# Two weight loads moved from SP's queue to GpSimd's in a one-core Mish feed-forward kernel

## The chip, the cores and the metric

The kernel runs on one core of a Trainium2 chip. The core has five engines with an instruction stream each: TensorE (PE, matmuls and, as PEld, their weight loads), VectorE (DVE), ScalarE (ACT), GpSimd (POOL) and SyncE (SP), which here only issues DMAs and waits. The engines run side by side and meet at semaphores. The metric is the device time of one execution in microseconds (us).

## The reference

With x of 2048 x 512, w1 of 512 x 1792 and w2 of 1792 x 512, all in bf16:

```
h   = einsum("bsd,df->bsf", x, w1) + b1
sp  = log1p(exp(-abs(h))) + where(h > 0, h, 0)      # softplus
act = h * tanh(sp)                                  # Mish
out = einsum("bsf,fd->bsd", act, w2)
```

So two matrix products with an elementwise Mish and a bias between them.

## The kernel before

**Tiles.** The 512 rows of w1 are 4 "k" tiles of 128, and the 1792 columns are 14 "f" tiles of 128. The 2048 tokens go in four blocks of 512 (BLOCKS), or 16 tiles of 128. The first product needs x with its 512 features on the partitions (xT) and gives h transposed: for each f tile, four matmuls over k collect in a bank of PSUM (line 192, `mm1_step`), and ACT applies Mish with the bias and writes a_sb (line 198). The second product takes a_sb as weights and w2 as the moving operand, 14 matmuls a token tile (line 249, `mm2`). ACT, or DVE for the last tile, copies the result out (lines 233 and 236), and a DMA stores it.

**Ten tokens apart.** For the last ten tokens (fewer f tiles of two of them) DVE computes h itself as 120 dot products (`dots`, line 211) from w1T and xv, with its own loads. ACT does their Mish late (line 223), just before the last token tile.

**The start.** PE opens with six dummy matmuls on constants (WARM, line 155). x's first two token tiles come in their natural layout (x_nat, one DMA each); PE transposes them against an identity (line 169), and DVE copies the result to xT (line 171). The identity is made by GpSimd: a memset of ones and one affine_select (lines 145 and 147). The rest of x arrives already transposed by the DMA. To have work early, PE goes through the first f tiles piece by piece, in the order of arrival:

```
transpose_x(0, ...)                 # x's token tile 0
first(0, 0)                         # k 0, f tiles 0-3, token tile 0
transpose_x(1, ...)                 # token tile 1
first(0, 1); first(1, 0); first(1, 1)
# then k 2 and 3 of f tiles 0-3, all k of f tiles 4-7, on token tiles 0-1 together;
# then token tiles 2-3 of f tiles 0-7, and from there whole blocks
```

`first(j, k)` is four matmuls of 128 columns. Each step waits for its own piece of w1 by a semaphore (`t_w1[k, f]`, in `mm1_step`), so an order that is fixed in the program meets loads that land when they land.

**Loads.** All are on line 92 of `load`, and the queue is the engine that issues: ACT issues k 0 of f tiles 0-3 and then b1; SP issues everything else, one after the other, in the order of the program. The first on SP are x_nat 0, x_nat 1, then k 1 (128 KB) and k 2-3 (256 KB) of f tiles 0-3, the two halves of f tiles 4-7 (256 KB each), the transposing load of tokens 256-511, the two halves of f tiles 8-13, w2, and then what DVE's dots and the later blocks need. Nothing on SP waits until the first store. The f tiles come in the groups (0, 4), (4, 8) and (8, 14) (GROUPS), and `load_w1(q, ks, a, b)` loads k range ks of f tiles a to b from queue q. GpSimd issues no DMA; it is done when the identity is.

Of the kernel before, what the change touches and what calls it, by code (L numbers as in the profile page):

```python
# [7 lines left out]
GROUPS = ((0, 4), (4, 8), (8, 14))  # L8
# [26 lines left out]
def bass_standalone__dense_activation_mish__prompt_kernel(  # L35
# [14 lines left out]
    KT, FT = D // P, F // P  # L50
# [7 lines left out]
    with ExitStack() as es:  # L58
# [22 lines left out]
        def sem(name):  # L81
            return es.enter_context(nc.semaphore(name))
# [5 lines left out]
        pool = Stream(nc.gpsimd, sem("c_pool"))  # L88

        def load(q, dst, src, name, transpose=False):  # L90
            s = sem(name)
            (q.eng.dma_start_transpose if transpose else q.eng.dma_start)(dst, src).then_inc(s, 16)  # L92
            return (s, 16)
# [3 lines left out]
        def load_w1(q, ks, a, b):  # L97
            t = load(q, w1_sb[:, ks, a * P:b * P], w1v[:, ks, a * P:b * P], "s_w1_%d_%d" % (ks.start, a))
            for f in range(a, b):
                for k in range(ks.start, ks.stop):  # L100
                    t_w1[k, f] = t
# [6 lines left out]
        def load_xT(lo, hi):  # L108
            t = load(sp, xT[:, :, lo:hi], x2[lo:hi, :], "s_xT%d" % lo, True)
            for j in range(lo // P, hi // P):  # L110
                t_xT[j] = t
# [15 lines left out]
        for a, b in GROUPS:  # L127
            if a == F0:
                load_xT(2 * P, 4 * P)
            for ks in (slice(0, 1), slice(1, 2), slice(2, KT)) if a == 0 else (slice(0, 2), slice(2, KT)):  # L130
                load_w1(act if (a, ks.start) == (0, 0) else sp, ks, a, b)
        t_b1 = load(act, b1_nat[:, :], b1.rearrange("(j p) -> j p", p=P), "s_b1")
        load_w2(0, 5)
# [8 lines left out]
        for s in range(2, len(BLOCKS)):  # L142
# [3 lines left out]
        pool.wait(t_ones)  # L146
        t_id = pool.mark(pool.eng.affine_select(ident[:, :], ones[:, :], pattern=[[1, P]], compare_op=ALU.is_equal,  # L147
                                                fill=0.0, base=0, channel_multiplier=-1))
        act.eng.preload_act_table(ACT.Mish)  # L149

        c_w = nc.const_aps.tensor(1.0, [P, P], BF)
# [177 lines left out]
```

## Time and profile before

| | us |
|---|---|
| median of 3 runs | 105.33 (105.02 to 105.4) |
| the profiled execution | 105.21 |
| its span, first to last instruction | 103.9 |
| PE busy | 100.9 |
| DVE busy | 77.1 |
| ACT busy | 48.1 |
| POOL busy | 0.7 |
| first matmul on k 1 of f tiles 0-3 | 5.16 from the span's start |

In the views of the profile, times count from the span's start. The timeline gives start and length; SPq and ACTq are the sequencers of SP and ACT issuing a DMA, and the length of such a row is the issue alone, not the transfer. The list of DMA issues gives the time from the start of the issue to the landing of the data, as a median where it groups several. In the table by stage, each row is a stretch, its length, the busy time of each engine with the count of instructions, the granted clock of TensorE, the mean busy share of the 16 DMA engines (which can count a little over 1) and what they moved in GB/s. The program calls w1 and w2 w_sb in these rows alike.

### The profile page before, as it was taken

The numbers are of one execution on the slowest core, as the hardware profiler recorded it, in microseconds if no ns is written. First come the engines' busy times: TensorE is split into PE (matmuls) and PEld (weight loads), VectorE is DVE, ScalarE is ACT, GpSimd is POOL, SyncE is SP. The second block draws the span as 40 slices with busy tenths as digits, with TensorE's granted clock in tenths as the row PEclk, the third lists the DMA queues.
The fourth block names the chain that finished last, engine by engine and source line by source line (L and its number), as shares of the span: only waits on it lengthen the run. The fifth ranks groups of instructions, "written<-read, shape, count | busy, mean of one in ns | idle before, by whom it ended". The sixth has DMA issues, their size and how long they took to land.

```text
span 103.9 us, 1471 instructions
## 1 busy us (share of the span) xinstructions
PE 100.9 (97%) x532; PEld 50.9 (49%) x532; DVE 77.1 (74%) x257; ACT 48.1 (46%) x75; POOL 0.7 (1%) x6
## 2 busy tenths in 40 slices
PE   6899999999999999999999999999999999999992
PEld 2598744444444444444444444444444444444482
DVE  0530000599999999999999999999999999990011
ACT  1303998112247777222227777522117778720220
POOL 2000000000000000000000000000000000000000
PEclk9999999999999999999999999999999999999999
DMA  2899999999999800010111000001111000001111
GB/s 76 244 304 349 348 367 188 357 289 207 154 244 250 266 8 0 0 50 2 48 50 50 3 0 6 3 0 50 50 50 50 0 0 0 0 6 50 50 50 51
DMA packets 21267, 11.11 MB, mean 107 GB/s; under 512 B 15372, under 2 KB 21004, under 8 KB 21260
## 3 DMA queue, kind: packets, MB, share of 16 engines
q1 hardware_dynamic: 20944, 10.86, 39.8%
q10 hardware_dynamic: 316, 0.16, 0.5%
q8 instruction: 4, 0.07, 0.3%
q14 instruction: 3, 0.02, 0.1%
HBM read 5.25 MB, written 2.10 MB: 71 GB/s over the span
## 4 chain that ended last, share of the span: by engine, by line
PE 93%; DMA 3%; SPq 1%; ACT 0%; issue 0%
PE ps L192 47%; PE ps L249 47%; DMA w_sb<-in_w_dram 3%; SPq L92 1%; ACT o_sb L233 0%
## 5 line engine op out<-in xcount | busy, mean ns | idle before, releaser
L211 DVE SCALAR_TENSOR_TENSOR prod<-w1T,xv 128x512 f32<-128x512 bf16 x120 | 73.6, 684 | 13.1 <-DMA w1T<-in_w_dram 13.1
L192 PE MATMUL ps<-xT,w_sb 128*128 128x512 bf16 (+4 forms) x264 | 49.6, 350 | 0.4 <-DMA w_sb<-in_w_dram 0.4
L249 PE MATMUL ps<-w_sb,a_sb 128*128 128x512 bf16 (+3 forms) x252 | 49.1, 355 | 0.0
L198 ACT ACTIVATE a_sb<-ps,b_sb 128x512 bf16<-128x512 f32 (+2 forms) x56 | 37.3, 691 | 14.0 <-PE ps L192 14.0
L192 PEld LDWEIGHTS ps<-xT,w_sb 128*128 128x128 bf16 x264 | 25.5, 100 | 23.7 <-DMA w_sb<-in_w_dram 0.7
L249 PEld LDWEIGHTS ps<-w_sb,a_sb 128*128 128x128 bf16 x252 | 23.6, 98 | 25.1
L233 ACT ACTIVATE o_sb<-ps 128x512 bf16<-128x512 f32 (+1 forms) x16 | 9.2, 576 | 38.2 <-PE ps L249 38.2
L211 DVE DVE_READ_ACCUMULATOR prod<-w1T,xv 128x1 f32 x120 | 9.6, 80 | 0.0
L236 DVE CAST o_sb<-ps 128x256 bf16<-128x256 f32 (+1 forms) x2 | 0.8, 375 | 7.7 <-PE ps L249 7.7
L155 PE MATMUL ps<-const-bfloat16-1.0 128*128 128x512 bf16 (+2 forms) x8 | 2.8, 498 | 0.8 <-PEq L314 0.8
L171 DVE COPY xT<-ps 128x128 bf16<-128x128 bf16 (+1 forms) x6 | 1.2, 245 | 2.9 <-PE ps L169 2.9
L149 ACT ACT_TABLE_LOAD x1 | 1.3, 1283 | 2.1 <-issue 2.1
L155 PEld LDWEIGHTS ps<-const-bfloat16-1.0 128*128 128x128 bf16 x8 | 1.0, 136 | 1.9 <-issue 1.9
L169 PE MATMUL ps<-ident,x_nat 128*128 128x128 bf16 x8 | 1.3, 311 | 0.0
L169 PEld LDWEIGHTS ps<-ident,x_nat 128*128 128x128 bf16 x8 | 0.9, 142 | 0.3 <-DMA x_nat<-in_x_dram 0.3
L273 DVE STREAM_TRANSPOSE b_t<-b_pad 32x32 bf16<-32x32 bf16 x4 | 0.8, 202 | 0.1
L123 DVE MEMSET b_pad<- 32x64 uint32 x1 | 0.1, 112 | 0.9 <-PEq L314 0.9
L219 DVE TENSOR_TENSOR hb<-hv,b_sb 128x40 f32<-128x40 f32 (+1 forms) x2 | 0.4, 218 | 0.1
L223 ACT ACTIVATE a_sb<-hb 128x40 bf16<-128x40 f32 (+1 forms) x2 | 0.4, 244 | 0.0
L147 POOL TENSOR_SCALAR_AFFINE_SELECT ident<-ones 128x128 bf16<-128x128 bf16 x1 | 0.3, 292 | 0.1
L145 POOL MEMSET ones<- 128x128 bf16 x1 | 0.2, 204 | 0.3 <-POOLq L314 0.3
L275 DVE CAST b_sb<-b_t 128x14 f32<-128x14 bf16 x1 | 0.2, 176 | 0.0
(5 smaller groups left out, 0.6 us busy)
## 6 DMA issues: line engine op xcount, KB each, us to landing
out_dram<-o_sb SPq DMA_DIRECT2D x15, 128.0 KB, 1.7
w_sb<-in_w_dram SPq DMA_DIRECT2D x1, 1152.0 KB, 10.5
w_sb<-in_w_dram SPq DMA_DIRECT2D x3, 256.0 KB, 4.0
w_sb<-in_w_dram SPq DMA_DIRECT2D x2, 384.0 KB, 4.7
xv<-in_x_dram SPq DMA_DIRECT2D x1, 768.0 KB, 7.9
w_sb<-in_w_dram SPq DMA_DIRECT2D x1, 640.0 KB, 6.4
xv<-in_x_dram SPq DMA_DIRECT2D x1, 512.0 KB, 11.0
x_nat<-in_x_dram SPq DMA_DIRECT2D x2, 128.0 KB, 2.3
```

What stands on the lines that cost most here:

```text
L92: (q.eng.dma_start_transpose if transpose else q.eng.dma_start)(dst, src).then_inc(s, 16)
L149: act.eng.preload_act_table(ACT.Mish)
L155: nc.tensor.matmul(ps[:, 3, 0:n], c_w, c_m[:, 0:n], start=True, stop=True)
L169: mm = nc.tensor.transpose(psb[:, i * P:(i + 1) * P], x_nat[:, j, k * P:(k + 1) * P], ident[:, :])
L171: t = dve.mark(nc.vector.tensor_copy(xT[:, ks[0]:ks[0] + n, j * P:(j + 1) * P], psb[:, 0:n * P].rearrange("p (k t) -> p k t", k=n)))
L192: return nc.tensor.matmul(ps[:, bank, lo:hi], w1_sb[:, k, f * P:(f + 1) * P], xT[:, k, starts[s] + lo:starts[s] + hi], start=first, stop=( ...
L198: t = act.mark(act.eng.activation(a_sb[:, f, starts[s]:starts[s] + width(s, f)], ps[:, bank, 0:width(s, f)], ACT.Mish, bias=b1_sb[:, f:f + ...
L211: t_dot[b] = dve.mark(nc.vector.scalar_tensor_tensor(prod[:, b, :], w1T[:, f, :], 1.0, xv[:, v, :], ALU.mult, ALU.mult, accum_out=hv[:, f, ...
L233: t = act.mark(act.eng.activation(o_sb[:, i, lo:hi], ps[:, bank, 0:hi - lo], ACT.Copy))
L236: t = dve.mark(nc.vector.tensor_copy(o_sb[:, i, lo:hi], ps[:, bank, 0:hi - lo]))
L249: mm = nc.tensor.matmul(ps[:, bank, 0:hi - lo], a_sb[:, f, i * P:(i + 1) * P], w2_sb[:, f, lo:hi], start=(f == 0), stop=(f == FT - 1))
L273: t_b1t = dve.mark(nc.vector.transpose(b1_t[c * 32:(c + 1) * 32, :], b1_pad[:, c * 32:(c + 1) * 32]))
```

## The change

The two loads of f tiles 0-3 behind k 0 are issued by GpSimd, behind the affine_select that makes the identity, instead of by SP.

```
         for a, b in GROUPS:
             if a == F0:
                 load_xT(2 * P, 4 * P)
-            for ks in (slice(0, 1), slice(1, 2), slice(2, KT)) if a == 0 else (slice(0, 2), slice(2, KT)):
+            for ks in (slice(0, 1),) if a == 0 else (slice(0, 2), slice(2, KT)):
                 load_w1(act if (a, ks.start) == (0, 0) else sp, ks, a, b)
...
         t_id = pool.mark(pool.eng.affine_select(ident[:, :], ones[:, :], pattern=[[1, P]], compare_op=ALU.is_equal,
                                                 fill=0.0, base=0, channel_multiplier=-1))
+        load_w1(pool, slice(1, 2), *GROUPS[0])
+        load_w1(pool, slice(2, KT), *GROUPS[0])
         act.eng.preload_act_table(ACT.Mish)
```

GpSimd's whole program in the changed kernel, in its order (w_sb 128x512 is k 1, w_sb 128x2x512 is k 2-3; lines behind the change count two more than before):

```order
L316 ISA
L316 MEMSET const-float32-0.0 128x1
L316 MEMSET const-float32-1.0 128x1
L316 MEMSET const-bfloat16-1.0 128x1
L316 MEMSET const-uint8-127 128x1
L145 MEMSET ones 128x128
L147 ISA
L147 AFFINE_SELECT ident<-ones 128x128
L92 DMA w_sb<-in_w_dram 128x512
L92 DMA w_sb<-in_w_dram 128x2x512
```

The last two rows are new; before, the program ended with the affine_select. They stand behind the mark that PE's transposes wait for.

SP's program at its start, as a difference (128x2x512 is k 2-3 of f tiles 0-3 and then each half of f tiles 4-7; 128x2x768 is a half of f tiles 8-13):

```order
 L92 DMA x_nat<-in_x_dram 128x512 x2
-L92 DMA w_sb<-in_w_dram 128x512
-L92 DMA w_sb<-in_w_dram 128x2x512 x3
+L92 DMA w_sb<-in_w_dram 128x2x512 x2
 L92 DMA_TRANSPOSE xT<-in_x_dram 128x4x256
 L92 DMA w_sb<-in_w_dram 128x2x768 x2
```

SP goes from x_nat straight to f tiles 4-7, and all its later loads stand two places further up. The order of every other engine stays as it was.

More of the change, by code (lines that the diff above doesn't have):

```diff
@@ L129, in bass_standalone__dense_activation_mish__prompt_kernel @@
                 load_xT(2 * P, 4 * P)
-            for ks in (slice(0, 1), slice(1, 2), slice(2, KT)) if a == 0 else (slice(0, 2), slice(2, KT)):
+            for ks in (slice(0, 1),) if a == 0 else (slice(0, 2), slice(2, KT)):
                 load_w1(act if (a, ks.start) == (0, 0) else sp, ks, a, b)
@@ L148, in bass_standalone__dense_activation_mish__prompt_kernel @@
                                                 fill=0.0, base=0, channel_multiplier=-1))
+        load_w1(pool, slice(1, 2), *GROUPS[0])
+        load_w1(pool, slice(2, KT), *GROUPS[0])
         act.eng.preload_act_table(ACT.Mish)
```

## The prediction

> **What bounds the kernel now.** I read the page's busy line and chain first, then the chain in order of time, then the timeline, the stage table and the DMA issues of the first 9 us.
>
> ```profile
> PE 100.9 (97%) x532; PEld 50.9 (49%) x532; DVE 77.1 (74%) x257; ACT 48.1 (46%) x75; POOL 0.7 (1%) x6
> PE 93%; DMA 3%; SPq 1%; ACT 0%; issue 0%
> ```
>
> ```profile
> 1.67 0.05 issue
> 1.72 3.40 DMA w_sb<-in_w_dram
> 5.12 0.04 issue
> 5.16 12.46 PE ps L192 x92
> 17.63 12.09 PE ps L249 x56
> ...
> 89.95 12.17 PE ps L249 x84
> 102.12 0.02 issue
> 102.14 0.25 ACT o_sb L233
> ```
>
> From 5.16 us to 102.12 us the chain is TensorE (PE) alone, one piece joined to the next. Before that stands one transfer: issued at 1.72 on SP's queue and landed 3.40 us later, at 5.12. Its place (the third issue of SP) makes it w1's k 1 of f tiles 0-3, the first of the two loads that move. So the change can act only on the moment at which PE gets going, and on stalls that it opens or closes soon after. The view of waits up to 20 us gives PE one stall for a load:
>
> ```profile
> PE ps L192 <- DMA w_sb<-in_w_dram: 0.4, 1, 0.4
> ```
>
> **Most that can be won.** In the timeline (start, length in us), cut to narrow windows, and in the table by stage of PE's line 192:
>
> ```profile
> 4.13 0.31 PE L169 MATMUL ps<-ident,x_nat 128*128 128x128 bf16 x1
> 4.13 0.63 PE L169 MATMUL ps<-ident,x_nat 128*128 128x128 bf16 x4
> 5.16 0.29 PE L192 MATMUL ps<-xT,w_sb 128*128 128x128 bf16 x1 [0.40 <-DMA w_sb<-in_w_dram]
> 5.16 0.61 PE L192 MATMUL ps<-xT,w_sb 128*128 128x128 bf16 x4 [0.40 <-DMA w_sb<-in_w_dram]
> 5.16:6.16 1.00, 1.00 (x12) 1.00 1.06 373
> 6.17:7.03 0.86, 0.86 (x11) 1.00 1.34 275
> 7.04:8.78 1.74, 1.74 (x18) 1.00 1.08 283
> ```
>
> The four transposes of x's second tile start (0.63 - 0.31) / 3 = 0.107 us apart, so the last starts at 4.45 and the next matmul could start at 4.55. The first matmul on k 1 starts at 5.16 instead: 0.61 us of starts are lost (0.40 in the profile's way of counting, from modelled end to start).
>
> Behind it come 12 matmuls of 128 columns (four on k 1, eight on x's second tile), and then, at 6.17, the first on k 2. The first of the 12 start (0.61 - 0.29) / 3 = 0.107 us apart, yet all 12 take 1.01 us, where 12 x 0.107 would be 1.28. PE doubles its pace in their midst, though the column of the granted clock says 1.00 throughout. Where PE starts at 4.55, two prices are possible. If the pace rises at the same moment as before, the 12 take 1.28 us and k 2 is wanted at 5.83: 0.34 us won. If it rises after the same work, k 2 is wanted at 4.55 + 1.01 = 5.56: 0.61 us won. I take 0.34, since the kernel's dummy matmuls start the work at the same moment in both, and keep 0.61 for the range. [...]
>
> **The change, part by part.** Removed from SP: two issues. Added to GpSimd, behind the identity: two. The rows of the issues:
>
> ```profile
> 1.07 0.29 POOL L147 TENSOR_SCALAR_AFFINE_SELECT ident<-ones 128x128 bf16<-128x128 bf16 x1
> 1.01 0.38 ACTq L92 DMA_DIRECT2D w_sb<-in_w_dram  x1
> 1.42 0.67 ACTq L92 DMA_DIRECT2D b_nat<-in_b_dram  x1
> 1.72 1.93 SPq L92 DMA_DIRECT2D w_sb<-in_w_dram  x4
> 3.69 1.30 SPq L92 DMA_TRANSPOSE xT<-in_x_dram  x1
> 7.49 2.27 SPq L92 DMA_DIRECT2D xv<-in_x_dram  x1
> ```
>
> GpSimd ends the identity at 1.36, and can begin at about 1.41 (ACT's second issue follows its first by 0.03, SP's by 0.05). PE waits for the identity itself and not for anything behind it, so that is untouched. Each SP issue takes 1.93 / 4 = 0.48 us, so everything behind the two moves up by some 0.95 us: the two halves of f tiles 4-7, the transposing load of x, and all later loads.
>
> How long a GpSimd issue takes, D, no row shows. The nearest rows are the same kind of load on other engines: 0.38 us on ACT is the lower end. The longest plain issue here, the broadcast of x at 2.27, is the upper. I take 1.0, near their geometric mean of 0.93, as the ends are far apart and neither is close in kind. The landing times after the issue are:
>
> ```profile
> w_sb<-in_w_dram ACTq DMA_DIRECT2D x1, 128.0 KB, 2.3
> w_sb<-in_w_dram SPq DMA_DIRECT2D x1, 128.0 KB, 3.4
> w_sb<-in_w_dram SPq DMA_DIRECT2D x1, 256.0 KB, 3.8
> w_sb<-in_w_dram SPq DMA_DIRECT2D x1, 256.0 KB, 4.0
> w_sb<-in_w_dram SPq DMA_DIRECT2D x1, 256.0 KB, 4.2
> xT<-in_x_dram SPq DMA_TRANSPOSE x1, 4.7
> ```
>
> *k 1.* ACT's load of k 0 (same size and shape, nothing ahead of it on its queue) lands 2.3 - 0.38 = 1.92 us after the end of its issue. So k 1 lands at 1.41 + D + 1.92: 3.7, **4.3** or 5.6 us for D of 0.38, 1.0 and 2.27. It is in time for PE's 4.55 up to D = 1.2, and earlier than before (5.12) up to D = 1.8.
>
> *k 2-3.* It is issued behind k 1 on GpSimd, and it is twice as large. Its 128 KB more cost 0.43 us at the 305 GB/s of the table below, or 0.86 at half of that, shared with SP's queue. So it lands about 1.41 + 2D + 1.92 + 0.65 = 3.98 + 2D: 4.7, **6.0** or 8.5 us. Before, it was the second of SP's four issues from 1.72, so issued at about 2.2, and landed by 6.0.
>
> The other limit on it is the transfer. All engines' stages:
>
> ```profile
> 0.00:3.50 3.50, 2.66 (x11) 1.25 (x12) 0.23 (x2) 1.28 (x1) 0.70 (x6) 1.00 0.49 137
> 3.50:4.25 0.75, 0.75 (x10) 0.64 (x8) 0.49 (x3) 0.00 (x0) 0.00 (x0) 1.00 0.56 83
> 4.25:5.25 1.00, 0.60 (x7) 0.33 (x6) 0.74 (x5) 0.00 (x0) 0.00 (x0) 1.00 0.94 305
> 5.25:6.25 1.00, 1.00 (x13) 1.00 (x14) 0.87 (x5) 0.00 (x0) 0.00 (x0) 1.00 1.08 378
> ```
>
> The last two columns are the DMA engines' busy share and GB/s. By 3.5 us 480 kB have moved, by 4.25 another 62 (a lull at 83 GB/s that no view explains), by 5.25 another 305. Before, k 2-3 stood ahead of f tiles 4-7 on one queue. Now these are issued at about 1.72 and 2.2, on another queue, and compete with it. If the two share evenly, k 1 and k 2-3 (393 kB) are through when x's first tile and k 0 (262 kB) and 393 kB from each of the two queues have moved, 1048 kB: 5.25 + (1048 - 847) / 378 = 5.8 us, or 0.55 earlier (62 kB in 0.75 us where 0.2 would do) if the lull does not come again. Before, the slowest of the 16 engines ended k 2-3 some 0.9 us after its bytes so counted (786 kB, reached at 5.05); with that lag it is 6.7. So 5.2 to 6.7 by this road, with the middle at 6.0, the value from the issues too. I take **6.0**.
>
> PE starts on k 1 at 4.55, is through with the 12 matmuls at 5.83, and waits 0.17 us for k 2-3. k 2 starts at 6.00 instead of 6.17: **0.17 us won**. The chain behind it: tiles 4-7 are wanted 0.86 us after k 2 (6.86) and had landed at about 2.66 + 4.0 = 6.7, their second half at 3.17 + 4.2 = 7.4 (wanted at 7.7), x's next 256 tokens at 3.69 + 4.7 = 8.4 (wanted at 8.6). All three are issued 0.95 us earlier, and the bytes ahead of them are the same in sum. Cost nothing; if they came no earlier than before, 0.15 us of cover would be left.
>
> VectorE's dots start and end earlier, but PE doesn't wait for them. The sum is 105.21 - 0.17 = 105.04 us for an execution like the profiled one (its 103.9 of span and 1.3 around it). The median of the runs is 0.12 above that execution, so **105.15 us**.
>
> [...]
>
> **Rivals.**
> *GpSimd's queue becomes the bound (slower).* k 2-3 pays D twice. From D = 1.35 it lands after 6.70, and PE is 0.53 us or more later than now. At D = 1.6 it is 7.2: 1.0 us lost, 106.4. At 2.27 it is 8.5: 107.7. For it: the dearest issues of the trace are over 1.35 us. Against it: the dearest one broadcasts four rows to each partition, where these load one and two, and SP's four plain issues took 0.48 each. With D spread evenly in ratio from 0.38 to 2.27, ln(2.27/1.35) / ln(2.27/0.38) = 0.29 lies above 1.35. Chance 0.30.
> *Transfers are the bound (a wash).* The bytes ahead of PE stay the same, the lull comes again, and k 2-3 loses to tiles 4-7 what it gains in issue: k 2 at 6.1 to 6.4, so 105.15 to 105.45 as executions go and 105.3 to 105.6 beside the median. For it: a DMA share near 1 from 4.25 on. [...] Against it: the share of 0.49 to 0.56 before. Chance 0.20.
> *Everything in time and the pace rises with the work (faster).* 0.61 us won, 104.7. Needs k 2-3 at 5.56, which asks for D under 0.8, and no lull. Chance 0.10.
> That the loads don't move can't be: the order of the changed program has them on GpSimd.
>
> **How the numbers follow.** The forecast (0 to 0.4 us won) has 0.40. Range: 104.7 (the faster rival) to 106.5 (D of about 1.7); above it lies ln(2.27/1.7) / 1.79 = 0.16, below it under 0.05. The likeliest case's own range is 104.9 to 105.4. A measurement here tells 0.5%, or 0.53 us, from nothing. Faster by that: only the third rival, 0.10. Slower: the first, 0.30. Within: the forecast and the wash, 0.60.
>
> **What would show it.** Two DMA rows on POOL, each about 1.0 us, the first at 1.4; k 1 landing by 4.55, with PE's starts unbroken from 3.0 to 5.8; then a wait of PE for the load of k 2-3, ended at about 6.0; SP's issue for the second half of f tiles 4-7 at about 2.2 instead of 3.2; and the same 97 us of PE behind it. Wrong it would be if a POOL row is over 1.35 us, or if PE waits for f tiles 4-7 or for x.

## The result and the profile after

The changed kernel takes 108.6 us (median of 4 executions, 107.78 to 109.36) against 105.37 before: a ratio of 1.030, with a 95% interval of 1.026 to 1.035. It is slower by 3.2 us, outside the predicted range of 104.7 to 106.5. The profiled execution is the slowest of the four, 109.36 us with a span of 108.1. (Some executions, of the kernel before too, come out over 1.5% above the fastest of the same kernel; the ratios leave these out, and no ratio is given where they are most of an experiment's executions.)

The page of the changed kernel, its busy line, its chain by engine and two of its DMA queues (packets, MB, share of the engines):

```profile
PE 103.5 (96%) x524; PEld 52.3 (48%) x532; DVE 77.1 (71%) x257; ACT 48.0 (44%) x75; POOL 2.1 (2%) x8
PE 88%; DMA 5%; ACT 3%; POOL 1%; issue 1%; ACTq 0%; POOLq 0%
q1 hardware_dynamic: 20528, 10.46, 37.3%
q0 software_dynamic: 128, 0.39, 1.4%
```

PE still makes up most of the chain, with 2.6 us more of busy time for the same matmuls: they went slower for a while. (The count of 524 against 532 is of records missing from this trace.) The two loads now have a queue of their own, q0, with 128 records for 0.39 MB. SP's queue has 416 records fewer for it (20944 before), and ACT's takes 416 more for the same two loads (732 against 316, in the run with ACT's loads below): the data go in 4 KB packets here, 96 of them, and in 1 KB packets there.

Its chain in order of time (start, length), PE's timeline in two narrow windows, and the landing times of the loads concerned:

```profile
1.44 0.71 POOL w_sb L92
2.15 5.68 DMA w_sb<-in_w_dram
7.83 0.05 issue
7.87 5.67 PE ps L194 x28
...
106.26 0.02 issue
```

```profile
5.39 1.46 PE L194 MATMUL ps<-xT,w_sb 128*128 128x128 bf16 x12 [0.50 <-DMA w_sb<-in_w_dram]
7.87 1.46 PE L194 MATMUL ps<-xT,w_sb 128*128 128x256 bf16 x6 [1.02 <-DMA w_sb<-in_w_dram]
```

```profile
w_sb<-in_w_dram SPq DMA_DIRECT2D x2, 256.0 KB, 5.5
w_sb<-in_w_dram POOLq DMA_DIRECT2D x1, 256.0 KB, 5.7
w_sb<-in_w_dram POOLq DMA_DIRECT2D x1, 128.0 KB, 3.9
```

GpSimd issues k 1 at 1.44 and k 2-3 at 2.15, 0.71 us each. k 1 lands at 5.3 (5.12 before), k 2-3 at 7.83 (6.0 before). PE starts on k 1 at 5.39, 0.22 late, and on k 2 at 7.87 instead of 6.17, 1.70 late. Its last matmul ends at 106.26 instead of 102.12: **4.14 us** late. So 2.44 us were lost behind k 2's start. PE waits for no load there:

```profile
PE ps L194 <- DMA w_sb<-in_w_dram: 1.5, 2, 1.0
```

These are the two waits ahead of k 1 and k 2 (0.50 and 1.02), and no other. What is lost behind them shows in PE's rows by stage, before and then after (stretch, length, busy time and count of matmuls):

```profile
8.00:9.00 1.00, 1.00 (x11) 1.00 1.06 318
9.00:10.00 1.00, 1.00 (x12) 1.00 1.05 367
```

```profile
9.00:10.00 1.00, 1.00 (x7) 1.00 1.10 387
13.00:14.00 1.00, 1.00 (x11) 1.00 1.11 350
```

The same matmuls of 256 columns go at 11 or 12 a microsecond before, and at 7 (with those that overlap an edge) after, until full pace returns; in the trace they start 0.109 us apart before (8 to 9 us) and 0.213 after (7.87 to 12.85). The trace's own record of the clock begins at 12.88 us here, at 5.89 before, and that is where the spacing changes. From 7.87 to 12.88 is 5.0 us at half pace, and half of it, 2.5 us, is lost.

### The profile page after: what moved, and what is told of

Its sections match the earlier page's. It is cut to its first block, busy times and chain, and to the rows that moved or that the text cites. A ratio compares the mean times of both kernels' runs of the same rounds, so it can differ in the third digit from the quotient of the medians.

```text
span 108.1 us, 1463 instructions
## 1 busy us (share of the span) xinstructions
PE 103.5 (96%) x524; PEld 52.3 (48%) x532; DVE 77.1 (71%) x257; ACT 48.0 (44%) x75; POOL 2.1 (2%) x8
## 4 chain that ended last, share of the span: by engine, by line
PE 88%; DMA 5%; ACT 3%; POOL 1%; issue 1%; ACTq 0%; POOLq 0%
PE ps L251 45%; PE ps L194 43%; DMA w_sb<-in_w_dram 5%; ACT a_sb L200 3%; POOL w_sb L92 1%; POOL ident L147 0%; ACT o_sb L235 0%; POOL ones L145 0%; ACTq L27 0%; POOLq L316 0%
## 5 line engine op out<-in xcount | busy, mean ns | idle before, releaser
L194 PE MATMUL ps<-xT,w_sb 128*128 128x512 bf16 (+4 forms) x261 | 52.3, 364 | 1.7 <-DMA w_sb<-in_w_dram 1.5
L251 PE MATMUL ps<-w_sb,a_sb 128*128 128x512 bf16 (+3 forms) x247 | 48.6, 355 | 0.3
L194 PEld LDWEIGHTS ps<-xT,w_sb 128*128 128x128 bf16 x264 | 27.0, 105 | 26.2 <-DMA w_sb<-in_w_dram 2.1
L92 POOL DMA_DIRECT2D w_sb<-in_w_dram x2 | 1.4, 713 | 0.1
```

Of the source, the lines that this page charges most:

```text
L194: return nc.tensor.matmul(ps[:, bank, lo:hi], w1_sb[:, k, f * P:(f + 1) * P], xT[:, k, starts[s] + lo:starts[s] + hi], start=first, stop=( ...
L251: mm = nc.tensor.matmul(ps[:, bank, 0:hi - lo], a_sb[:, f, i * P:(i + 1) * P], w2_sb[:, f, lo:hi], start=(f == 0), stop=(f == FT - 1))
```

## The experiments

Three theories stood at the outset. *Queue theory:* a load issued by GpSimd is late as such. *Transpose theory:* the transposing load of x, which SP now issues 0.95 us earlier, holds up the end of k 2-3. *Pace theory:* the 2.44 us are a consequence of PE's gaps, not of a load. A fourth, *sharing theory*, was formed after the first four runs: two queues share the DMA engines, so that what PE wants first no longer comes first.

### The changed kernel once more

> The changed kernel once more, for a second profile. In the first, k 1 landed at 5.34 us and k 2-3 at 7.82, PE began k 2 at 7.87 instead of 6.17, and then went at half pace to 12.9 us; the span grew by 4.2 us, 1.7 of it by k 2's start and 2.4 behind it. Queue theory (GpSimd's loads as such are late): k 1 at 5.3 and k 2-3 at 7.8 again, within 0.3. Transpose theory (the end of k 2-3 is told late because the transposing load of x, issued 0.95 us earlier now, is under way on the same DMA engines): k 2-3's end falls together with the end of the load of f tiles 4-7's second half again. Pace theory (the 2.4 us are PE's half pace, kept up by PE's gaps, and depend on where a gap falls): the lateness of k 2 stays near 1.7, but the moment of full pace moves from run to run, anywhere from 9 to 13 us, and the span with it, from 106 to 108.1.

Measured: 108.69 us, span 107.4. PE's timeline and its rows by stage:

```profile
6.11 0.84 PE L194 MATMUL ps<-xT,w_sb 128*128 128x128 bf16 x12 [1.32 <-DMA w_sb<-in_w_dram]
8.06 1.25 PE L194 MATMUL ps<-xT,w_sb 128*128 128x256 bf16 x5 [1.11 <-DMA w_sb<-in_w_dram]
```

```profile
6.11:6.95 0.84, 0.84 (x12) 1.00 1.55 301
8.06:9.06 1.00, 0.99 (x5) 0.50 1.18 320
9.06:10.06 1.00, 1.00 (x7) 0.50 1.05 370
12.00:13.00 1.00, 1.00 (x12) 1.00 1.10 345
```

k 1 is later than in the first profile (6.06), k 2-3 about the same (8.0; k 2 starts 1.89 late). The column of the granted clock now shows the half pace: PE was at full pace for the 12 small matmuls, and at 0.50 in the stages from 8.06 on, until 11.4. The loss behind k 2's start is 1.6 us instead of 2.4. The lateness repeats; the pace moves from execution to execution, as pace theory has it.

### The transposing load held back a little

```
             if a == F0:
+                sp.wait(t_xn[1])
                 load_xT(2 * P, 4 * P)
```

> As the changed kernel, but SP waits for x's second natural tile (landed at 3.8 us) before it issues the transposing load of x, so that this load goes out at about 3.9 as in the kernel before (3.69) instead of at 2.72. Transpose theory: k 2-3 lands by about 6.5 instead of 7.8, PE begins k 2 at about 6.7, 1.2 us earlier, and the time falls by at least 1.2 us, to 107.4 or below. Queue theory: k 2-3 lands at 7.8 as before the edit, and the time stays at 108.6 or rises a little, since x's tokens come later.

Measured: 107.32 us (106.51 to 109.36), a ratio of 1.015 (1.006 to 1.023). The time is under the 107.4 that transpose theory asked for, but the profile, taken of the execution of 109.36, does not show its reason: the transposing load goes out at 3.80, and k 2-3 lands 5.4 us after its issue, at 7.57, not at 6.5. Transpose theory in this form misses: x's packets move from 6.3 us on here, 5.9 in the changed kernel, ahead of k 2-3's last ones all the same.

### The same loads from ACT

```
-            for ks in (slice(0, 1),) if a == 0 else (slice(0, 2), slice(2, KT)):
-                load_w1(act if (a, ks.start) == (0, 0) else sp, ks, a, b)
+            for ks in (slice(0, 1), slice(1, 2), slice(2, KT)) if a == 0 else (slice(0, 2), slice(2, KT)):
+                load_w1(act if a == 0 else sp, ks, a, b)
...
-        load_w1(pool, ...)      # both
```

> The same two loads, in the same place ahead of SP's, but issued by ACT behind its load of k 0 (and ahead of b1) instead of by GpSimd. Queue theory: k 1 lands at about 4.2 and k 2-3 at about 5.5, PE's gap ahead of k 1 goes, and the time is 0.2 to 0.5 us under the kernel before, about 105.0. Transpose theory: k 1 comes early here too, but k 2-3 still ends with the transposing load that SP issues 0.95 us earlier, at 7 to 7.8, and the time is 107 to 108.6.

Measured: 106.48 us once and 108.72 to 109.26 in the three other executions; the profile is of one of the three (109.06). The loads of ACT (the second row is the one issued at 1.43, the first that at 1.91):

```profile
w_sb<-in_w_dram ACTq DMA_DIRECT2D x1, 256.0 KB, 6.7
w_sb<-in_w_dram ACTq DMA_DIRECT2D x1, 128.0 KB, 4.6
```

k 1 lands at 6.05 and k 2-3 at 8.65, later than from GpSimd. Queue theory falls, as far as this profile goes: with another issuing engine the loads are as late. The two runs with SP's other loads held back, one with GpSimd's loads and one with ACT's, bear it out below. What the two kernels have in common is that SP's loads for f tiles 4-7 and x are issued 0.95 us earlier, beside them.

### Dummy matmuls in PE's gaps

```
+        def fill(n):
+            pe.wait(*free[4])
+            nc.tensor.matmul(ps[:, 4, 0:n], c_w, c_m[:, 0:n], start=True, stop=True)
+        fill(512)
         first(0, 1)
         first(1, 0)
         first(1, 1)
+        for _ in range(3):
+            fill(512)
```

> As the changed kernel, with PE's two gaps filled by dummy matmuls of 512 columns on constants (one ahead of k 1, three ahead of k 2, 0.43 us each at half pace), loads untouched. Pace theory: full pace comes by 6 to 9.5 us instead of 12.9, so of the 2.4 us behind k 2's start 1.2 to 2.4 go, and the time is 106.2 to 107.4. If the lateness behind k 2 has another cause (late loads of the later f tiles, ACT), the time stays at 108.6 or rises by what the dummies add.

Measured: 106.83 us (106.52 to 107.41), a ratio of 1.011 (1.008 to 1.014). The profile's rows of PE, start and pace:

```profile
8.36 1.05 PE L194 MATMUL ps<-xT,w_sb 128*128 128x256 bf16 x8 [0.50 <-DMA w_sb<-in_w_dram]
8.40:9.40 1.00, 1.00 (x10) 1.00 1.15 315
9.40:10.40 1.00, 1.00 (x12) 1.00 1.06 372
```

Though k 2 starts even later here, at 8.36 (2.19 late), PE goes at full pace from there, and the whole loss in the profile is those 2.19 us. Of the 3.2 us between the medians, about 1.8 go with dummy work on constants that touches no load. Pace theory holds against its rivals, late loads or ACT. The dummies do not close the gaps, though: both loads land later still here, and 1.00 us without work is left ahead of k 1 and 0.50 ahead of k 2. At k 1 (6.37) PE is already at full pace, as it was early in five other profiles (last section), so that the dummies brought it there rests on the times of all six executions and not on this profile.

### One load alone

```
-            for ks in (slice(0, 1),) if a == 0 else ...
+            for ks in (slice(0, 1), slice(2, KT)) if a == 0 else ...     # k 1 alone on GpSimd
+            for ks in (slice(0, 1), slice(1, 2)) if a == 0 else ...      # k 2-3 alone on GpSimd
```

In each, GpSimd keeps the one matching call of `load_w1`.

> Only k 1 moves to GpSimd; k 2-3 stays on SP, right behind x's second natural tile. Sharing theory (every load that SP issues earlier shares the DMA engines with the loads on the other queue, so what PE wants first no longer comes first): k 1 now shares with k 2-3 and lands at 5.0 to 6.0, no earlier than before; k 2-3 is still ahead of f tiles 4-7 on its queue and lands at 5.3 to 6.2; PE begins k 2 at 6.2 to 7.0, and the time is 105.3 to 107, depending on whether PE reaches full pace. Queue theory: k 1 at 5.3 to 6, k 2-3 at 5.5, and the time follows k 1 alone, 105.5 to 106.5. This run tells mostly what moving the first load alone costs.

> Only k 2-3 moves to GpSimd; k 1 stays on SP behind x's second natural tile. Sharing theory: k 1 lands at about 5.1 as before, or a little sooner; k 2-3 shares with f tiles 4-7 and lands at 7 to 8; PE begins k 2 at 7 to 8, and the time is 106.5 to 108.6: most of the loss comes from this load. If the loss came from k 1, k 2-3 would land by 6.3 and the time be 105.2 to 105.6.

Measured: with k 1 alone 105.48 us (105.23 to 107.5), a ratio of 1.003 (0.999 to 1.007), no difference. With k 2-3 alone 106.17 us once and 107.77 to 107.94 in the three other executions; the profile is of one of the three. The loads, first of k 1 alone, then of k 2-3 alone:

```profile
w_sb<-in_w_dram SPq DMA_DIRECT2D x1, 256.0 KB, 4.5
w_sb<-in_w_dram POOLq DMA_DIRECT2D x1, 128.0 KB, 4.2
```

```profile
w_sb<-in_w_dram POOLq DMA_DIRECT2D x1, 256.0 KB, 4.6
w_sb<-in_w_dram SPq DMA_DIRECT2D x1, 128.0 KB, 4.5
```

With k 1 moved alone it lands at 5.6, half a microsecond later than from SP, and k 2-3 on SP at 6.3 instead of 6.0; PE, at full pace early in this execution, ends 0.18 us late. With k 2-3 moved alone the expectation of a late k 2-3 was wrong: it lands at 6.0, on time, and k 1, still on SP and issued at the same moment as before, lands at 6.2 instead of 5.1. PE starts on k 1 1.09 us late and then goes at half pace to about 10 us; PE's last matmul ends 2.6 us late. So in each run a load is late that the other queue's load moved beside, on GpSimd's queue in the first and on SP's in the second. That agrees with sharing theory, but which load loses it does not say, and k 2-3 shared too and lost nothing.

### SP's other loads held back

```
             if a == 4:
+                sp.wait(t_xn[1])        # or t_xn[0], below
```

> As the changed kernel, both loads on GpSimd, but SP waits for x's second natural tile (landed at 3.8) before it issues f tiles 4-7 and all behind them, so that nothing on SP's queue shares the DMA engines with the two loads until about 4.8. Sharing theory: k 1 lands at 4.5 to 5.3 and k 2-3 by 5.5 to 6.3; PE begins k 2 at or before the 6.17 of the kernel before; then PE waits for f tiles 4-7 or for x's tokens, 1 to 2 us in all, since these are 2 us late: 105.5 to 107. Queue theory: k 1 and k 2-3 land at 5.3 and 7.8 as in the changed kernel, and the time is 108.6 or more.

Measured: 106.03 us (105.53 to 106.75), a ratio of 1.008 (1.005 to 1.011). Two landings, and PE's rows:

```profile
w_sb<-in_w_dram POOLq DMA_DIRECT2D x1, 256.0 KB, 3.2
w_sb<-in_w_dram POOLq DMA_DIRECT2D x1, 128.0 KB, 3.3
```

```profile
4.76 2.27 PE L196 MATMUL ps<-xT,w_sb 128*128 128x128 bf16 x20
7.35 5.01 PE L196 MATMUL ps<-xT,w_sb 128*128 128x256 bf16 x44 [0.32 <-DMA w_sb<-in_w_dram]
```

With SP's other loads held to 3.61 us, the same two loads from GpSimd land at 4.7 and 5.4 instead of 5.3 and 7.8. PE's gap ahead of k 1 is gone, and the 20 matmuls behind it, up to the last on k 2-3, run through. This is the gain that the change could have had; it is given back in a wait of 0.32 us for f tiles 4-7, which SP now issues at 3.6. Sharing theory holds: 2.6 of the 3.2 us between the medians are gone, and 0.65 (106.03 against 105.38) is left. This run holds back f tiles 4-7 and the transposing load together; the next one tells the two apart.

### The transposing load behind k 2-3

```
+        # the making of the identity and GpSimd's two loads stand ahead of SP's loads in the text
             if a == F0:
+                sp.wait(t_w1[2, 0])
                 load_xT(2 * P, 4 * P)
```

> As the changed kernel, but SP waits until k 2-3 has landed before it issues the transposing load of x; f tiles 4-7 are issued early as in the changed kernel. Transpose theory, in its narrower form (k 2-3's data are through by 6.1 to 6.9, but its last completions are told only when the transposing load on the same DMA engines is done): k 2-3 lands by 6.4 to 7.2 instead of 7.6 to 8.3, PE begins k 2 by 7.2, and then waits for x's tokens, which come at about 11. Sharing theory alone: k 2-3 lands at 7.5 or later as before. The time is no reading here, since x's tokens come some 2 us late.

Measured: 107.26 us, a ratio of 1.020 (1.012 to 1.027), with x's tokens late as foreseen. f tiles 4-7 are issued as early as in the changed kernel, and still:

```profile
w_sb<-in_w_dram POOLq DMA_DIRECT2D x1, 256.0 KB, 4.7
6.88 2.79 PE L196 MATMUL ps<-xT,w_sb 128*128 128x256 bf16 x24 [0.28 <-DMA w_sb<-in_w_dram]
10.30 2.14 PE L196 MATMUL ps<-xT,w_sb 128*128 128x256 bf16 x18 [0.62 <-DMA xT<-in_x_dram]
```

k 2-3 lands at 6.84, and PE starts on k 2 at 6.88 instead of 7.87 to 8.36. The trace's semaphore updates, 16 for each load, as many as there are DMA engines, show how (last ones, us):

```
k 2-3, changed kernel, first profile   ... 6.33 6.45 6.45 | 7.83
k 2-3, changed kernel, second profile  ... 6.94 6.96 7.02 | 7.89 7.89 8.02
f tiles 4-7, second half, first profile    6.09 | 7.73 7.73 ... 7.84 7.85
k 2-3, transposing load behind it      ... 6.74 6.78 6.84
```

In the changed kernel 15 or 13 of the 16 reports on k 2-3 have come by about 7.0. The others come 0.9 to 1.4 us later, together with f tiles 4-7's second half, whose own reports all but one come in a bunch at 7.73 to 7.85. What is late there is the report and not the data: the last packet on GpSimd's queue ends at 6.16 in the first profile and at 6.96 in the second. With the transposing load kept away, no such bunch comes. (The kernel before has the bunch too, at 7.32 to 7.39, but there all of k 2-3 had been reported by 5.96.) So of the 1.70 us by which PE begins k 2 late in the first profile, 0.99 go with the transposing load, and they are one to three reports of 16 that come late; the other 0.71 stay, with f tiles 4-7 still beside the two loads. This split comes from one profile of each kernel. Transpose theory's narrower form holds; that the late reports come from the engines on which the transposing load had begun is inferred, as the trace does not name the engine of a report. The first attempt, the hold to 3.8, missed since it moved x's packets by 0.4 us only. By what rule a report is held back, no run shows.

### The kernel before, with its gap filled and with a stall

```
+        pe.wait(*free[4])
+        nc.tensor.matmul(ps[:, 4, 0:512], c_w, c_m[:, 0:512], start=True, stop=True)
         first(0, 1)
```

> The kernel before, with one dummy matmul of 512 columns on constants (0.43 us at half pace) in PE's gap ahead of k 1. Pace theory: the gap before k 1 is what sometimes keeps PE at half pace; filled, full pace comes no later than before, the runs near 107 that the kernel before has go, and the median is 105.0 to 105.4. If the gap plays no part, the times are those of the kernel before, the runs near 107 included.

Measured: 105.41 us (104.83 to 106.23), a ratio of 1.002 (0.998 to 1.005): no difference, and no execution near 107 among its 12. The kernel before had 4 near 107 among its 28 beside them, and 10 among all its 59; at that rate about one set of 12 in nine has none by chance. The gap is not closed either: k 1 lands at 5.55 in this profile, and 0.90 us without work is left. So it stays open whether the gap plays a part in the executions near 107, and none of them was traced.

```
+        pe.wait(t_xT[2])
         for a, b in GROUPS[:2]:
```

> The kernel before with its loads untouched, but PE waits for the transposing load of x (landed at 8.4) before its first matmul on k 2, so that k 2 starts about 2.3 us later, at about 8.5. All loads that PE wants next have landed by then. Pace theory: on top of the 2.3 us, PE falls to half pace for a stretch of about 3.4 us, 1.7 us lost, in most executions: 108.5 to 109.5. If a late k 2 costs only itself: 107.6 to 107.8.

Measured: 109.75 us (108.83 to 110.3), a ratio of 1.039 (1.031 to 1.046). The transposing load landed later in this profile (9.6), so k 2 starts 3.47 us late. PE by stage:

```profile
9.64:10.64 1.00, 0.99 (x5) 0.50 1.05 372
10.64:11.64 1.00, 1.00 (x7) 0.50 1.09 368
13.00:14.00 1.00, 1.00 (x12) 1.00 1.10 349
```

The loads are those of the kernel before, all landed, and PE falls to a granted clock of 0.50 in its gap of 3.2 us; the trace's record has 0.50 from 9.35 to 12.76. The last matmuls are 4.99 us late, 1.5 more than the stall itself. A late load here costs itself and then half of what is left of a stretch of 3.41 us: PE works from 9.64 to 12.76 at half pace, 3.12 us, and half of that is 1.56.

### A shorter hold, and the hold with ACT

> As the changed kernel, but SP waits for x's first natural tile (landed at 2.9) before it issues f tiles 4-7 and all behind. Between the changed kernel, which issues them at 1.7, and the hold behind the second tile, issued at 3.6 with 0.35 us lost at f tiles 4-7. Sharing theory: k 1 lands at 4.6 to 5.1, k 2-3 at 5.4 to 6.2, f tiles 4-7 by 7.0 and 7.6, the tokens of x by 8.6; PE waits little anywhere, and the time is 105.0 to 105.6. Should sharing begin to bite, k 2-3 lands after 6.2 and the time is 106 or more.

> The two loads on ACT behind k 0, and SP holds f tiles 4-7 and all behind until x's second natural tile has landed (3.8). Beside the same hold with GpSimd's loads (k 1 at 4.7, k 2-3 at 5.4, 106.0): if GpSimd's way of loading costs nothing of its own, k 1 lands at 4.3 to 4.8 and k 2-3 at 5.2 to 5.5, and the time is 105.8 to 106.2. If it does cost, both land 0.5 us or more earlier here.

Measured: with SP's wait for x's first natural tile, 105.32 us (104.92 to 105.74), a ratio of 0.9995 (0.997 to 1.002): the loss of the changed kernel is gone, and no gain is there. k 1 lands at 5.1 and k 2-3 at 5.8; PE runs from 5.18 to 7.78 without a break, begins k 2 at 5.87 (0.30 earlier than before), and gives its lead back in a wait for the second half of f tiles 4-7:

```profile
5.18 2.60 PE L196 MATMUL ps<-xT,w_sb 128*128 128x128 bf16 x28 [0.29 <-DMA w_sb<-in_w_dram]
7.97 6.22 PE L196 MATMUL ps<-xT,w_sb 128*128 128x256 bf16 x46 [0.19 <-DMA w_sb<-in_w_dram]
```

With ACT's queue and the longer hold, 106.03 us, a ratio of 1.006 (1.003 to 1.009), k 1 lands at 4.5 and k 2-3 at 5.4, beside 4.7 and 5.4 from GpSimd. GpSimd's way of loading costs 0.2 us at most in these two profiles. No version here beats the kernel before.

## Why the prediction was wrong

**Right.** The bound and the place: PE is the bound, all its waits for loads lie ahead of k 2, and behind that it waits for none. SP's second issue for f tiles 4-7 went out at 2.2 as foreseen. The issue on GpSimd was cheaper than taken (D 0.71 against 1.0), so by the formula 3.98 + 2D, k 2-3 should have landed at 5.4 and the change have won its 0.34 us. With SP's loads held back it did land at 5.4, in part by luck: by the same working k 1 would have come at 4.04 and k 2-3 1.36 behind it, and they came at 4.72 and 0.67 behind it.

**Wrong: "I take 6.0" for k 2-3.** It landed at 7.8 and 8.0. The step had two roads. The issue road gave 4.7 to 8.5 with D as the unknown, and D was not the cause. The transfer road counted bytes with an even share and gave 5.2 to 6.7. Its upper end allowed 0.9 us for the slowest engine, as measured in the kernel before, where the transposing load came too late to touch k 2-3 (its first packet moved at 6.01, and k 2-3 was reported by 5.96). It had no term for a report that the transposing load holds up, and this made 1.0 of the 1.7 us. Without it, in the run with the transposing load behind k 2-3, the load lands at 6.84, just above that road's upper end of 6.7.

**Wrong: k 1 at 4.3, from ACT's load with "nothing ahead of it on its queue".** It landed at 5.3 and 6.1: nothing ahead on its queue is not nothing beside it. Held apart from SP's loads it came at 4.7, still 0.4 us after my value, and 0.7 after what the formula gives with the measured D. The lull of the last section does not explain it: the run with ACT's loads and SP held back has next to none, and by the same working k 1 would come at 1.88 + 1.92 = 3.80 there and came at 4.54. What moved beside it in both runs are k 0 and x's tiles, which no run holds back, so the cause of this rest stays open.

**Wrong: the moved-up loads "cost nothing".** f tiles 4-7 and x, 0.95 us earlier, were the cost. I looked at whether PE would wait for them and not at whom they would delay.

**Wrong: that PE's pace "rises at the same moment as before".** It rose 7 us later in the first profile. I priced only earlier work, 0.34 or 0.61 us won; a gap that keeps PE at half pace stood in no term. It made 2.44 of 4.14 us in the profile, and 1.8 of 3.2 between the medians by the run with dummies in the gaps.

**The rivals.** "Transfers are the bound" had the mechanism at a small part of its price: k 2 at 6.1 to 6.4, when it was 7.87, and without the pace. "GpSimd's queue becomes the bound" had the sign, and its cause is refuted by ACT's runs. The chance of 0.30 for slower and the upper end of 106.5 rested on D alone; a k 2-3 made late by SP's loads had no part in either.

## What to carry to other kernels

A queue is also an order: from SP's one queue the loads landed here in the order in which PE wants them (k 1 at 5.12, k 2-3 at 5.96, f tiles 4-7 at 6.70 and 7.39). Moving the first two to a second queue let what stood behind them start 0.95 us earlier, beside them, and k 2-3 landed at 7.83 (5.4 with SP's other loads held back). Ask which transfers are moved up, and whom they delay, above all a transposing load, which here held up the report of a load that was all but done (7.83 with it, 6.84 with it kept behind). Where PE goes at half pace behind a gap, as here, price a late load as its lateness plus half of the time that PE then works at half pace (2.4 and 1.5 us in two profiles), or put dummy work into the gap (1.8 us won here).

## What was not expected of the hardware

**Pace.** PE's full pace came at 5.89 us before (with a gap of 0.40 us in the profile), at 12.88 and 13.26 with gaps of 0.50 and 0.62 us ahead of k 1 and a second one ahead of k 2, and at 5.95 and 6.57 with no gap. The kernel with the stall had it at 5.94 in spite of a gap of 0.54 ahead of k 1, so the length of the gap does not decide alone. In five other profiles it was there by 3.9 to 4.7, ahead of any gap, so where a gap falls against the start of the full pace differs from one execution to the next. The trace's record shows it lost again for a stretch of 3.41 us: 0.50 from 7.98 to 11.39 in the second profile of the changed kernel, and from 9.35 to 12.76 in the kernel with the stall. Why both have that length, no run shows. The granted clock in the tables of the first profiles reads 1.00 for stretches in which the count of matmuls shows half pace (7 of them from 9 to 10 us in the changed kernel): its record begins only at 12.88 there.

**A lull.** From about 3.1 to 4.6 us, 5 to 16 packets of w1 behind k 0 took 0.4 to 1.3 us each (1 KB takes 0.05 us otherwise, 4 KB 0.16) in each of the 14 profiles but one, on SP's, ACT's or GpSimd's queue; with ACT's loads and SP held back it was one packet. What it comes from stays open. So does why, with k 2-3 alone on GpSimd, SP's k 1 lost and not k 2-3; GpSimd's packets are of 4 KB and SP's of 1 KB, which no run varied.
